# Attention forward and backward on one core: another hand-written order of units, other engines for some copies, 20 transposes ahead, last stores in halves

## The chip, the core and the metric

The kernel runs on one core of a Trainium2 chip. A core has a matrix engine (TensorE, "PE" in the profile; its weight loads are "PEld"), three engines for element-wise work (VectorE "DVE", ScalarE "ACT", GpSimd "POOL"), a queue engine that here does nothing but issue transfers (SyncE, "SP"), and sixteen DMA engines that carry out those transfers between the chip's HBM and the core's SBUF. Every transfer of this kernel is spread over all sixteen, eight partitions of a tile to each. TensorE writes to PSUM, 128 partitions by eight banks of 512 fp32 columns; VectorE and ScalarE read PSUM, GpSimd and the DMA engines don't.

The metric is the device time of one launch in microseconds. The kernel before takes 672.28 us, the median of eight runs.

## The reference, cut to what matters

Grouped-query attention for 32 batches, 32 query heads, 4 key/value heads, 4 queries per head, 2048 keys, head size 128, and its three gradients for a given output gradient:

```python
B, Hq, Hkv, Sq, Sk, D = 32, 32, 4, 4, 2048, 128

def _fwd_reference(q, k, v):
    k = jnp.repeat(k, rep, axis=1)          # rep = Hq // Hkv = 8
    v = jnp.repeat(v, rep, axis=1)
    scores = jnp.einsum("bhqd,bhkd->bhqk", q, k) * D ** -0.5
    p = jax.nn.softmax(scores, axis=-1)
    return jnp.einsum("bhqk,bhkd->bhqd", p, v)

def reference(q, k, v, grad_out):
    _out, _vjp = jax.vjp(_f, q, k, v)
    return (_out, *_vjp(grad_out))          # out, dq, dk, dv
```

The eight query heads of a key/value head, times four queries, are 32 rows; four key/value heads make 128 rows, one per partition. All arrays are bf16. Per batch K, V, dK and dV are 2 MiB each, the rest is small: 256 MiB of K, V, dK, dV plus 4 MiB of q, output gradient, output and dq cross the DMA engines, 260 MiB.

## The kernel before, in words

**Data.** On the host K and V are laid out as two arrays each, one for heads 0-1 and one for heads 2-3; a row of one partition holds 4096 bf16 values. K's rows carry 128 more, the q rows in the first array and the output gradient in the second (`LONG` = 4224 against `ROW` = 4096). So a batch loads four tiles, LK0, LK1 (1056 KB each), LV0, LV1 (1024 KB), and stores four, SV0, SV1 (dV) and SK0, SK1 (dK), of which SV1 and SK1 carry the output and dq in their last 128 columns. All tiles live in 20 SBUF buffers, `row0` to `row19` ("slots"), used for loads and stores alike. A load into a slot waits until the store from it has landed, or until TensorE has read the load that was there.

**Units.** The program is a list of units, each a short group of instructions of one engine. For a batch: transposes of q and the output gradient (QT, L230) and their copy out of PSUM (QTe); transposes of K and V, eight groups of four fp32 transposes each (KT, VT, L241: two neighbouring bf16 values travel as one fp32), and their copies to SBUF (KTe, VTe: ScalarE at L207, VectorE at L209); scores (S, L255, two halves into four banks); negative maximum (MX, VectorE, L260); exponential with row sums (EX, ScalarE, L264); reciprocal (RC, L268); three small GpSimd products (dop, qp, rs, L271 to L278); transposes of the exponentials (ET) and copies (ETe); output (O, L288) and its scaling (Oe, L294/L296); delta (DL, L299); DP (L255) and dS (DS, VectorE, L303); transposes of dS (DT, DTe); dq (DQ, L288, DQe L294/L296); dV and dK, eight units each, two matmuls into two banks (DV, DK, L310), and their casts into the store tiles (DVe, DKe, L316, ScalarE or VectorE).

**Order.** `PLAN` is one long string, four characters to a unit: the unit's kind (a letter, see `NAMES`), its part, its place (a PSUM bank, a slot, or "A"/"D" for ScalarE/VectorE) and a tile number. `plan()` reads it, counts the occurrences of a letter and part to get the batch, and `emit` writes the instructions in exactly that order under a manual schedule. Every engine works through its own units strictly in this order, and so does SyncE with the transfers: a transfer that must wait holds back all that follow it. The eight transfer semaphores are used in turn, so transfer n also waits until transfer n-8 has landed. The batches overlap: around the transposes of one batch stand dV and dK of the one before it, and loads run about three batches ahead.

In the middle of the run SyncE's order before is, for one batch, LK0.13, SK1.9, SV1.10, LV0.12, SV0.10, LK1.13, SK0.10, LV1.13 (kind, part, batch). Its end is LK0.31, SK1.27, SV1.28, LV0.30, SV0.28, LK1.31, SK0.28, LV1.31, SK1.28, SV1.29, LV0.31, and then eleven stores: SV0.29, SK0.29, SK1.29, SV1.30, SV0.30, SK0.30, SK1.30, SV1.31, SV0.31, SK0.31, SK1.31. The first batch's four loads are issued in halves (L225), heads first, in the order LK0, LK1, LV1, then LK0 of batch 1, LV0.

Of the kernel before, what the change touches and what calls it, by code (L numbers as in the profile page):

```python
# [14 lines left out]
P = 128  # L15
NH = 4
# [5 lines left out]

NAMES = dict(
# [5 lines left out]
    "a000a110b120a030b040a150e400f4A0e011f0A0e702f7A0e513f5A0b160a070e224f2A0e135f1D0c000d0D0e316f3A0g720h7A0e637f6A0"  # L29
    "b080a190g601h6D0g212h2A0i040i1-0j0D0g303h3A0e411f4A0e024f0A0g104h1D0k0A0g415h4D0g026h0D0l0D0e705f7A0e516p020q0A0"  # L30
    "f5D0b1a0p131q1D0m0-0A340B3A0A060B0D0A100B1A0a0d0r020r1-0s0D0t0D0o0-0A640B6A0A760B7D0u020v0D0g502h5A0A540B5A0E1c0"
    "b0e0A460B4A0e210f2D0e102f1D0c020d0D0e333f3A0A240B2A0E0b0u160v1D0g703h7A0e617f6A0n0-0C020D0D0C140D1A0C360D3D0a1h0"
    "g604h6A0g216h2A0i021i1-0j0D0C200D2A0g360h3A0e470f4A0w100x1A0k0A0g111h1D0g462h4D0g075h0D0C400D4D0w061x0A0l0D0e072"
    "f0A0C620D6A0F0f0C740D7D0e763f7A0e504p010q0A0f5D0b1i0p171q1D0m0-0A320B3A0A040B0D0A100B1A0a040r060r1-0s0D0t0D0A720"
    "B7D0o0-0A640B6A0u061v0D0g500h5A0y010C540D5A0y1-0z0D0F1g0A520B5A0E120b0c0A460e201f2A0B4D0e115f1D0c040d0D0e356f3A0"
    "A220B2A0E0j0u160v1D0g701h7A0e617f6A0n0-0C040D0D0C120D1A0C360D3D0a180g605h6A0g216h2A0i020i1-0j0D0C200D2A0g360h3A0"
    "e471f4A0w101x1A0g112h1D0k0A0g463h4D0g074h0D0C400D4D0w060x0A0l0D0e072f0A0C620D6A0F060C740D7D0e765f7A0e506p010q0A0"
    "f5D0b100p171q1D0m0-0A320B3A0A040B0D0A100B1A0a0g0r060r1-0s0D0t0D0o0-0A620B6A0A740B7D0y070C500D5A0y1-0z0D0F1b0u020"
    "v0D0g560h5A0A540B5A0E1f0b020A400B4D0e270f2A0e163f1A0c020d0D0e334f3D0A240B2A0E010u100v1D0g722h7A0e637f6A0n0-0C060"
    "D0D0C140D1A0C300D3D0a130g624h6A0g236h2A0i041i1-0j0D0C220D2A0g300h3A0C720e410f4A0w100x1A0g111h1D0k0A0g403h4D0g015"  # L40
    "h0D0C440D4A0w001x0D0l0D0D7A0e012f0D0C660D6A0F0a0e743f7D0e504p020q0A0f5D0b150p111q1D0m0-0A340B3A0A060B0D0A120B1A0"
    "a0b0r000r1-0s0D0t0D0o0-0A640B6A0A760B7D0y010C520D5A0y1-0z0D0F1j0u041v0D0g500h5A0A560B5A0E160b0f0A420B4D0e211f2A0"
    "e105f1A0c040d0D0e356f3D0A260B2A0E0e0u120v1D0g711h7A0e607f6A0n0-0C040D0D0C160D1A0C320D3D0a170g615h6A0g206h2A0i040"
    "i1-0j0D0C200D2A0g320h3A0e431f4A0w101x1A0g112h1D0k0A0g423h4D0g034h0D0C400D4D0w020x0A0l0D0e032f0A0C640D6A0F0i0C760"
    "D7D0e725f7A0e506p010q0A0f5D0b190p131q1D0m0-0A340B3A0A060B0D0A100B1A0a0j0r020r1-0s0D0t0D0o0-0A640B6A0A760B7D0y030"
    "C500D5A0y1-0z0D0F110u040v0D0g520h5A0A560B5A0E1a0b060A400B4D0e230f2A0e123f1A0c040d0D0e354f3D0A260B2A0E0c0u100v1D0"
    "g732h7A0e627f6A0n0-0C040D0D0C160D1A0C300D3D0a1h0g634h6A0g226h2A0i041i1-0j0D0C220D2A0g300h3A0e410f4A0w120x1A0g131"
    "h1D0k0A0g403h4D0g015h0D0C420D4D0w001x0A0l0D0e012f0A0C640D6A0F000C760D7D0e703f7A0e514p020q0A0f5D0b1e0p131q1D0m0-0"
    "A340B3A0A060B0D0A100B1A0a010r020r1-0s0D0t0D0o0-0A640B6A0A760B7D0y030C500D5A0y1-0z0D0F1d0u041v0D0g520h5A0A560B5A0"
    "E1i0b0a0A400B4D0e231f2A0e125f1A0c040d0D0e356f3D0A260B2A0E020u100v1D0g731h7A0e627f6A0n0-0C040D0D0C160D1A0C300D3D0"  # L50
    "a180g635h6A0g226h2A0i040i1-0j0D0C220D2A0g300h3A0e411f4A0w121x1A0g132h1D0k0A0g403h4D0g014h0D0C420D4D0w000x0A0l0D0"
    "e012f0A0C640D6A0F050C760D7D0e705f7A0e516p020q0A0f5D0b1f0p131q1D0m0-0A340B3A0A060B0D0A100B1A0a0d0r020r1-0s0D0t0D0"
    "o0-0A640B6A0A760B7D0y030C500D5A0y1-0z0D0F140u040v0D0g520h5A0A560B5A0E100b090A400B4D0e230f2A0e123f1A0c040d0D0e354"
    "f3D0A260B2A0E0c0u100v1D0g732h7A0e627f6A0n0-0C040D0D0C160D1A0C300D3D0a1g0g634h6A0g226h2A0i041i1-0j0D0C220D2A0g300"
    "h3A0e410f4A0w120x1A0g131h1D0k0A0g403h4D0g015h0D0C420D4D0w001x0A0l0D0e012f0A0C640D6A0F0i0C760D7D0e703f7A0e514p020"
    "q0A0f5D0b160p131q1D0m0-0A340B3A0A060B0D0A100B1A0a040r020r1-0s0D0t0D0o0-0A640B6A0A760B7D0y030C500D5A0y1-0z0D0F130"
    "u041v0D0g520h5A0A560B5A0E150b0e0A400B4D0e231f2A0e125f1A0c040d0D0e356f3D0A260B2A0E020u100v1D0g731h7A0e627f6A0n0-0"
    "C040D0D0C160D1A0C300D3D0a1b0g635h6A0g226h2A0i040i1-0j0D0C220D2A0g300h3A0e411f4A0w121x1A0g132h1D0k0A0g403h4D0g014"
    "h0D0C420D4D0w000x0A0l0D0e012f0A0C640D6A0F000C760D7D0e705f7A0e516p020q0A0f5D0b1a0p131q1D0m0-0A340B3A0A060B0D0A100"
    "B1A0a030r020r1-0s0D0t0D0o0-0A640B6A0A760B7D0y030C500D5A0y1-0z0D0F170u040v0D0g520h5A0A560B5A0E1i0b0f0A400B4D0e230"  # L60
    "f2A0e123f1A0c040d0D0e354f3D0A260B2A0E0c0u100v1D0g732h7A0e627f6A0n0-0C040D0D0C160D1A0C300D3D0a190g634h6A0g226h2A0"
    "i041i1-0j0D0C220D2A0g300h3A0e410f4A0w120x1A0g131h1D0k0A0g403h4D0g015h0D0C420D4D0w001x0A0l0D0e012f0A0C640D6A0F0h0"
    "C760D7D0e703f7A0e514p020q0A0f5D0b150p131q1D0m0-0A340B3A0A060B0D0A100B1A0a070r020r1-0s0D0t0D0o0-0A640B6A0A760B7D0"
    "y030C500D5A0y1-0z0D0F1j0u041v0D0g520h5A0A560B5A0E100b060A400B4D0e231f2A0e125f1A0c040d0D0e356f3D0A260B2A0E020u100"
    "v1D0g731h7A0e627f6A0n0-0C040D0D0C160D1A0C300D3D0a1e0g635h6A0g226h2A0i040i1-0j0D0C220D2A0g300h3A0e411f4A0w121x1A0"
    "g132h1D0k0A0g403h4D0g014h0D0C420D4D0w000x0A0l0D0e012f0A0C640D6A0F010C760D7D0e705f7A0e516p020q0A0f5D0b1i0p131q1D0"
    "m0-0A340B3A0A060B0D0A100B1A0a0j0r020r1-0s0D0t0D0o0-0A640B6A0A760B7D0y030C500D5A0y1-0z0D0F180u040v0D0g520h5A0A560"
    "B5A0E1h0b0a0A400B4D0e230f2A0e123f1A0c040d0D0e354f3D0A260B2A0E0c0u100v1D0g732h7A0e627f6A0n0-0C040D0D0C160D1A0C300"
    "D3D0a1f0g634h6A0g226h2A0i041i1-0j0D0C220D2A0g300h3A0e410f4A0w120x1A0g131h1D0k0A0g403h4D0g015h0D0C420D4D0w001x0A0"
    "l0D0e012f0A0C640D6A0F0d0C760D7D0e703f7A0e514p020q0A0f5D0b100p131q1D0m0-0A340B3A0A060B0D0A100B1A0a080r020r1-0s0D0"  # L70
    "t0D0o0-0A640B6A0A760B7D0y030C500D5A0y1-0z0D0F1g0u041v0D0g520h5A0A560B5A0E110b050A400B4D0e231f2A0e125f1A0c040d0D0"
    "e356f3D0A260B2A0E020u100v1D0g731h7A0e627f6A0n0-0C040D0D0C160D1A0C300D3D0a160g635h6A0g226h2A0i040i1-0j0D0C220D2A0"
    "g300h3A0e411f4A0w121x1A0g132h1D0k0A0g403h4D0g014h0D0C420D4D0w000x0A0l0D0e012f0A0C640D6A0F040C760D7D0e705f7A0e516"
# [87 lines left out]
def kernel(  # L161
# [36 lines left out]
    for u in units:  # L198
        if u.name in ("SV", "SK"):
            T[u.b]["D" + u.name[1], "out", u.part] = slots[int(u.where, 36)]  # L200
# [161 lines left out]
```

## Time and profile before, and how to read it

| | us |
|---|---|
| median of 8 runs (671.21 to 675.53) | 672.28 |
| the profiled execution, whole | 672.37 |
| its span (first to last instruction on the core) | 669.8 |
| TensorE busy / share | 610.2 / 91% |
| VectorE busy / share | 571.7 / 85% |
| ScalarE busy / share | 569.5 / 85% |
| GpSimd busy / share | 39.0 / 6% |
| HBM read / written | 136.31 MB / 136.31 MB |

Times in the profile count from the start of the span. Busy time is the union of an engine's instructions, so an engine can be busy nearly all the time and still not be what sets the end; a matmul's end is modelled. "PEclk" is the clock that TensorE was granted, in tenths of full speed. The costliest groups of the page, as line, engine, operation, out<-in, shapes, count | busy us, mean ns of one | idle before it, and what ended that:

```profile
L241 PE MATMUL psum<-ident,row 128*128 128x128 f32 x2048 | 292.0, 285 | 27.3 <-DMA row<-in_k_dram 19.5
L316 ACT CAST row<-psum 128x1024 bf16<-128x1024 f32 x292 | 289.5, 1024 | 31.2 <-PE psum L310 29.3
L316 DVE CAST row<-psum 128x1024 bf16<-128x1024 f32 x220 | 265.0, 1218 | 6.7 <-PE psum L310 3.8
L207 ACT COPY kt_sb<-psum 128x512 f32<-128x512 f32 x190 | 110.5, 599 | 21.4 <-PE psum L241 21.2
L303 DVE SCALAR_TENSOR_TENSOR ds_sb<-psum,delta,e_sb 128x1024 bf16<-128x1024 f32 x64 | 82.1, 1283 | 12.2 <-PE psum L255 7.5
```

The transfers, by what they write and read, with the size and the median time from issue to landing:

```profile
out_dram<-row SPq DMA_DIRECT2D x64, 1056.0 KB, 20.1
out_dram<-row SPq DMA_DIRECT2D x64, 1024.0 KB, 20.4
row<-in_k_dram SPq DMA_DIRECT2D x62, 1056.0 KB, 18.0
row<-in_v_dram SPq DMA_DIRECT2D x62, 1024.0 KB, 20.5
```

And what SyncE waited for, in total, times, longest:

```profile
SPq L320 <- DMA out_dram<-row: 124.1, 63, 2.2
SPq L226 <- DMA out_dram<-row: 106.1, 23, 5.6
SPq L320 <- DVE row L316: 87.2, 15, 9.7
SPq L226 <- DMA row<-in_v_dram: 83.6, 45, 2.1
```

### The profile page before, as it was taken

What the parts mean: (1) busy time and instruction counts of PE and PEld (TensorE: products, weight loads), DVE (VectorE), ACT (ScalarE), POOL (GpSimd) and SP (SyncE); (2) the same over time, 40 slices, a digit from 0 to 9 for tenths busy, and PEclk for the clock granted to TensorE, in tenths of its full rate; (3) what the DMA queues carried; (4) which work ended last, traced back from release to release, by engine and by line L of the source; (5) the groups of instructions that cost most, each with busy time, mean ns of one, the idle gap of its engine ahead of it and who ended that gap; (6) DMA issues with size and microseconds to landing.
All of it is one profiled execution on the core that took longest, in us unless ns stands there. A gap on an engine that the chain in (4) does not pass through costs nothing.

```text
span 669.8 us, 20678 instructions
## 1 busy us (share of the span) xinstructions
PE 610.2 (91%) x8768; PEld 403.8 (60%) x8768; DVE 571.7 (85%) x736; ACT 569.5 (85%) x802; POOL 39.0 (6%) x102
## 2 busy tenths in 40 slices
PE   6998999999998999989998989988999988898994
PEld 5665666666665666666655666655656665565652
DVE  1988899999997999979898889988789988887994
ACT  3987899999897899879888888987788988887894
POOL 0000000000000000000000000000000000000000
PEclk9999999999998999989999999999899999998997
DMA  9999999999999999999999999999999999999867
GB/s 352 420 423 422 427 400 421 423 424 423 424 425 424 423 425 424 423 425 419 408 420 424 413 413 409 408 420 421 417 420 412 416 419 422 399 421 424 353 251 322
DMA packets 37532, 273.96 MB, mean 409 GB/s; under 512 B 4160, under 2 KB 4160, under 8 KB 5184
## 3 DMA queue, kind: packets, MB, share of 16 engines
q1 hardware_dynamic: 37440, 272.65, 98.3%
q8 instruction: 68, 1.11, 0.6%
q14 instruction: 24, 0.20, 0.1%
HBM read 136.31 MB, written 136.31 MB: 407 GB/s over the span
## 4 chain that ended last, share of the span: by engine, by line
DMA 44%; PE 42%; ACT 5%; DVE 4%; issue 3%; SPq 0%; POOL 0%; DVEq 0%; ACTq 0%; POOLq 0%
DMA out_dram<-row 25%; PE psum L241 22%; DMA row<-in_k_dram 19%; PE psum L310 9%; PE psum L288 5%; PE psum L255 5%; ACT row L316 4%; DVE vt_sb L209 3%; DVE ds_sb L303 1%; DVE row L316 0%; PE psum L230 0%; ACT e_sb L264 0%; DVE e_sb L260 0%; ACT kt_sb L207 0%; ACT dt_sb L207 0%
## 5 line engine op out<-in xcount | busy, mean ns | idle before, releaser
L241 PE MATMUL psum<-ident,row 128*128 128x128 f32 x2048 | 292.0, 285 | 27.3 <-DMA row<-in_k_dram 19.5
L316 ACT CAST row<-psum 128x1024 bf16<-128x1024 f32 x292 | 289.5, 1024 | 31.2 <-PE psum L310 29.3
L241 PEld LDWEIGHTS psum<-ident,row 128*128 128x128 f32 x2048 | 226.5, 144 | 92.6 <-issue 32.6
L316 DVE CAST row<-psum 128x1024 bf16<-128x1024 f32 x220 | 265.0, 1218 | 6.7 <-PE psum L310 3.8
L207 ACT COPY kt_sb<-psum 128x512 f32<-128x512 f32 x190 | 110.5, 599 | 21.4 <-PE psum L241 21.2
L207 ACT COPY vt_sb<-psum 128x512 f32<-128x512 f32 x160 | 92.1, 603 | 33.8 <-PE psum L241 33.1
L303 DVE SCALAR_TENSOR_TENSOR ds_sb<-psum,delta,e_sb 128x1024 bf16<-128x1024 f32 x64 | 82.1, 1283 | 12.2 <-PE psum L255 7.5
L310 PE MATMUL psum<-ds_sb,qp_sb 32*128 32x512 bf16 x512 | 77.4, 386 | 3.4 <-ACT row L316 1.0
L260 DVE TENSOR_SCALAR_CACHE_REDUCE e_sb<-psum 128x2048 bf16<-128x2048 f32 x32 | 73.3, 2292 | 5.7 <-PE psum L255 5.7
L310 PE MATMUL psum<-e_sb,dop_sb 32*128 32x512 bf16 x512 | 69.0, 386 | 2.5 <-issue 1.1
L209 DVE COPY vt_sb<-psum 128x1024 bf16<-128x1024 bf16 x96 | 60.7, 684 | 10.3 <-PE psum L241 10.1
L209 DVE COPY kt_sb<-psum 128x1024 bf16<-128x1024 bf16 x66 | 45.0, 684 | 27.4 <-PE psum L241 27.1
L264 ACT ACTIVATE e_sb<-psum,m 128x2048 bf16<-128x2048 f32 x32 | 64.1, 2002 | 0.2 <-DVE e_sb L260 0.2
L271 POOL TENSOR_SCALAR dop_sb<-row,rinv 128x128 bf16<-128x128 bf16 x32 | 19.3, 602 | 603.9 <-DVE rinv L268 586.2
L241 PE MATMUL psum<-ident,ds_sb 128*128 128x128 f32 x256 | 42.2, 288 | 9.5 <-DVE vt_sb L209 7.0
L288 PE MATMUL psum<-row,dt_sb 128*32 128x128 bf16 x2048 | 44.0, 224 | 4.7 <-issue 4.6
L310 PEld LDWEIGHTS <-qp_sb 32*128 32x128 bf16 x512 | 19.4, 91 | 46.3 <-issue 42.9
L255 PE MATMUL psum<-vt_sb,qdt_sb 128*32 128x512 bf16 x512 | 40.1, 382 | 4.1 <-issue 4.1
L288 PEld LDWEIGHTS <-dt_sb 128*32 128x32 bf16 x2048 | 31.3, 96 | 20.8 <-issue 20.2
L241 PEld LDWEIGHTS psum<-ident,ds_sb 128*128 128x128 f32 x256 | 27.0, 141 | 27.2 <-DVE vt_sb L209 16.4
L207 ACT COPY dt_sb<-psum 128x512 f32<-128x512 f32 x63 | 38.3, 609 | 1.0 <-PE psum L241 0.9
L288 PEld LDWEIGHTS <-et_sb 128*32 128x32 bf16 x2048 | 30.4, 95 | 13.4 <-ACT et_sb L207 11.2
(29 smaller groups left out, 310.0 us busy)
## 6 DMA issues: line engine op xcount, KB each, us to landing
out_dram<-row SPq DMA_DIRECT2D x64, 1056.0 KB, 20.1
out_dram<-row SPq DMA_DIRECT2D x64, 1024.0 KB, 20.4
row<-in_k_dram SPq DMA_DIRECT2D x62, 1056.0 KB, 18.0
row<-in_v_dram SPq DMA_DIRECT2D x62, 1024.0 KB, 20.5
row<-in_v_dram SPq DMA_DIRECT2D x4, 512.0 KB, 9.6
row<-in_k_dram SPq DMA_DIRECT2D x2, 544.0 KB, 5.4
row<-in_k_dram SPq DMA_DIRECT2D x2, 512.0 KB, 4.5
```

Source lines behind the costliest of these rows:

```text
L207: nc.scalar.copy(out=out.bitcast(FP32), in_=in_)
L209: nc.vector.tensor_copy(out=out, in_=in_.bitcast(BF16))
L241: nc.tensor.transpose(out=ps[:, P * j:P * j + P], in_=src[:, 4 * half + j, :], identity=ident32[:])
L255: nc.tensor.matmul(out[r, QW * w:QW * w + QW], lhsT=t["qdt"][:, P * side + 32 * h:P * side + 32 * h + 32], rhs=t[x, NH * i + h][:, QW * w: ...
L260: nc.vector.tensor_scalar(out=t["e"][:], in0=t["S"], scalar1=-scale, scalar2=None, op0=ALU.mult, op1=ALU.min, accum_out=t["m"][:])
L264: nc.scalar.activation(out=t["e"][:], in_=t["S"], func=ACT.Exp, bias=t["m"][:], scale=scale, accum_out=t["l"][:])
L271: nc.gpsimd.tensor_scalar(out=t["dop"][:], in0=t["go"], scalar1=t["rinv"][:], scalar2=None, op0=ALU.mult)
L288: nc.tensor.matmul(t[name][r, :], lhsT=left[:, j, r, odd], rhs=right[:, 4 * i + j, :, odd], start=(i == 0 and c == 0), stop=(i == 1 and c ...
L303: nc.vector.scalar_tensor_tensor(out=t["ds"][:, w], in0=t["DP", i], scalar=t["dl"][:], in1=t["e"][:, w], op0=ALU.subtract, op1=ALU.mult)
L310: nc.tensor.matmul(acc[:, QW * (h % 2):QW * (h % 2) + QW], lhsT=t[still][rows[h], :], rhs=t[moving][rows[h], QW * i:QW * i + QW], start=Tr ...
L316: copy(out=heads_of(t[name[:2], "out", g])[:, :, QW * i:QW * i + QW], in_=t[name[:2], i, g].rearrange("p (h c) -> p h c", h=2))
```

## The change

The buffers, the tiles, the number and kind of units (but for the last stores) and the mathematics stay as they are. Five things change.

1. `PLAN` is another order. Units are moved one by one, on all engines. SyncE's order in the middle of the run becomes LK0.13, SK1.9, SV1.10, LK1.13, LV0.12, LV1.13, SV0.10, SK0.10. Its start is LK0.0, LV0.0, LK1.0, LV1.0, LK0.1, LK1.1, LK1.2, LK0.2, LV1.1, LK0.3, LV1.2, LV0.1, LV0.2, and only then the first store, SV0.0. Its end is LV0.30, SV0.28, LK1.31, SK1.27, SK1.28, LV1.31, LV0.31, SK0.28, SV1.28, SV1.29, SK0.29, SV0.29, SV0.30, SV1.30, SK0.30, SK1.29 and the last batch's stores with SK1.30 among them.
2. Copies out of PSUM change engines. For O and dq (Oe, DQe) 41 of 64 go from VectorE to ScalarE; V transposes' copies move by three to VectorE, K's by one to ScalarE, dK's casts by one to VectorE.
3. The store tiles have another layout, which the host undoes: a cast writes one run of 1024 columns where it wrote two runs of 512.
4. Twenty transposes of the identity come first on TensorE, into bank 7, which nothing reads.
5. The last batch's four stores are issued as two halves each (parts 2 to 5 of SV and SK); the first batch's loads are no longer split.

```diff
+LAST = 31
+WARM_UP = 20
...
 PLAN = (
-    "a000a110b120a030b040a150e400f4A0e011f0A0e702f7A0e513f5A0b160a070e224f2A0e135f1D0c000d0D0e316f3A0g720h7A0e637f6A0"
...
+    "F1c0u021v0D0g500h5A0A560B5A0E530A440B4D0A200B2D0E4a0E2a0u120v1D0C060D0D0C140D1A0C300D3A0C220D2A0w050x0A0w141x1A0"
+    "C400D4D0C660D6A0F290F3i0F490C720D7D0y040y1-0o0-0z0D0C500D5A0F5i0")
...
         u.name, u.part, u.b = NAMES[key[0]], int(key[1]), seen[key]
+        if u.name in ("SV", "SK") and u.part > 1:
+            u.b = LAST
...
         if u.name in ("SV", "SK"):
-            T[u.b]["D" + u.name[1], "out", u.part] = slots[int(u.where, 36)]
+            T[u.b]["D" + u.name[1], "out", u.part % 2] = slots[int(u.where, 36)]
...
-    heads_of = lambda row: row[:, 0:ROW].rearrange("p (h c) -> p h c", h=2)
...
-            for w in (slice(0, Sk), slice(Sk, n)) if b == 0 else (slice(0, n),):
-                nc.sync.dma_start(out=x[:, w], in_=src[:, w])
+            nc.sync.dma_start(out=x[:, 0:n], in_=src)
...
-            copy(out=heads_of(t[name[:2], "out", g])[:, :, QW * i:QW * i + QW],
-                 in_=t[name[:2], i, g].rearrange("p (h c) -> p h c", h=2))
+            copy(out=t[name[:2], "out", g][:, 2 * QW * i:2 * QW * i + 2 * QW], in_=t[name[:2], i, g])
         elif name in ("SV", "SK"):
-            n = LONG if i else ROW
-            nc.sync.dma_start(out=(dv_r if name == "SV" else dk_r)[i][b], in_=t["D" + name[1], "out", i][:, 0:n])
+            half, g = divmod(i, 2)
+            n = LONG if g else ROW
+            w = (slice(0, n), slice(0, ROW // 2), slice(ROW // 2, n))[half]
+            nc.sync.dma_start(out=(dv_r if name == "SV" else dk_r)[g][b][:, w], in_=t["D" + name[1], "out", g][:, w])
 
     with tc.manual_schedule():
+        for _ in range(WARM_UP):
+            nc.tensor.transpose(out=psum[:, QW * (BANKS - 1):QW * (BANKS - 1) + P], in_=ident32[:], identity=ident32[:])
         for u in units:
             emit(u)
...
-    return x.reshape(2, 32, P, 2, 8, P, 2).transpose(1, 0, 3, 5, 4, 6, 2).reshape(32, NH, 16 * P, P)
+    return x.reshape(2, 32, P, 4, 2, 2, P, 2).transpose(1, 0, 4, 6, 3, 5, 7, 2).reshape(32, NH, 16 * P, P)
```

## The prediction

> **What bounds the kernel now.** I read the page's slices first, then the chain of waits, the TensorE timeline, windows of the tail, and last the DMA view of ten microseconds near the end.
>
> ```profile
> DMA  9999999999999999999999999999999999999867
> GB/s 352 420 423 422 427 400 421 423 424 423 424 425 424 423 425 424 423 425 419 408 420 424 413 413 409 408 420 421 417 420 412 416 419 422 399 421 424 353 251 322
> ...
> q1 hardware_dynamic: 37440, 272.65, 98.3%
> ```
>
> The DMA engines have work in every slice but the last three. In the chain of waits, long stretches are nothing but transfers, end to end:
>
> ```profile
> 546.26 20.44 DMA out_dram<-row
> ...
> 566.78 20.51 DMA out_dram<-row
> ...
> 587.37 20.47 DMA out_dram<-row
> ```
>
> A link is 20.5 us because at most eight transfers are in flight: SyncE issues transfer n when n-8 has landed (a load landed at 584.70, the eighth after it was issued at 584.76). Eight transfers are one batch, so a batch takes 20.5 us. TensorE waits for that:
>
> ```profile
> 543.74 1.07 PE L241 MATMUL psum<-ident,row 128*128 128x128 f32 x8 [1.50 <-DMA row<-in_k_dram]
> 584.83 1.07 PE L241 MATMUL psum<-ident,row 128*128 128x128 f32 x8 [1.56 <-DMA row<-in_k_dram]
> ```
>
> Some 1.5 us per batch of compute slack. The end looks different:
>
> ```profile
> 620.00:630.00 10.00, 9.64 (x90) 6.75 (x87) 9.59 (x12) 9.45 (x16) 1.20 (x3) 1.00 0.93 392
> 630.00:640.00 10.00, 9.61 (x196) 5.65 (x196) 8.80 (x14) 8.71 (x13) 0.00 (x0) 1.00 0.82 335
> 640.00:650.00 10.00, 9.25 (x136) 6.11 (x137) 9.45 (x11) 9.44 (x14) 1.20 (x3) 1.00 0.48 197
> 650.00:660.00 10.00, 8.82 (x142) 4.19 (x142) 8.74 (x12) 9.31 (x12) 0.00 (x0) 0.91 0.84 344
> 660.00:670.00 10.00, 1.92 (x58) 1.10 (x46) 1.09 (x2) 1.44 (x2) 0.00 (x0) 0.67 0.64 265
> ```
>
> The DMA share (column before the last) leaves 0.7 + 1.8 + 5.2 + 1.6 + 3.6 = 12.9 us free, which reads as what earlier loads could win. The same 640 to 650 in quarter-microseconds says otherwise:
>
> ```profile
> DMA  9997999977999111000000000200000020009779
> GB/s 371 540 473 329 394 394 492 524 295 328 426 524 492 33 66 66 34 0 34 34 34 0 34 34 34 66 34 34 34 0 34 34 67 34 0 34 493 295 295 459
> ```
>
> From 643 to 649 one packet of 8 KB moves per 0.25 us: one engine of sixteen works off a backlog. The trace keeps an arrival event per engine and transfer, and they say the same: the store issued at 637.0 reached half its engines at 641.4 and the last at 650.3. This last engine falls behind all along: 1.9 us after the first at 50 us, 5.7 at 150, 13 from 320 on. Its arrivals from 150 to 625 us are apart, in the median, 2.45 us for a 1 MiB load, 2.59 for a 1 MiB store; the first engine's are 2.42 and 2.46. Its last arrivals are 628.21, 630.66, 633.77, 636.59, 638.99, 642.40, 644.73, 647.33, 650.25, 653.16, 655.72, 658.33, 661.10, 663.74, 666.18, 668.69: no hole in it. So the bound is this one late engine, from its first arrival (4.40) to its last (668.69): 664.3 us for 259.5 MiB, 2.56 us per MiB.
>
> The Trainium skill, "DMA: Bandwidth & Descriptors" (Latency and other measured facts), says engines 7 and 15 are usually slower, guesses at the descriptor rings of GpSimd's software path, and excludes the hardware path. The page's queue 1 is hardware and an engine is late, so the row decides; by the rule all engines would keep the first engine's pace, about 260 x 2.45 = 637 us, and the tail would count.
>
> **The change, part by part**, as microseconds on that engine. The run profiled took 672.37: span 669.8 (1.1 after the last arrival) and 2.6 around it; the median of eight is 672.28. I add to the median.
>
> *Bytes.* Same 260 MiB in 260 transfers (eight half loads fewer, four whole ones more; eight half stores for four whole). 0.
>
> *Order of the queue.* K heads 2-3 (LK1) move up by 1 to 3 MiB in most batches, V mostly by 1 to 4, dV/dK stores mostly back, by up to 4. Load after load goes from 39 pairs to 70, store after store from 39 to 74. On the late engine a 1056 KB load takes 2.551 after a load and 2.525 after a store; a 1056 KB store 2.679 after a store and 2.706 after a load. 31 x 0.026 - 31 x 0.027 = 0.
>
> *Loads close behind the store that frees their slot.* Before, never fewer than 7 places; after, 15 loads stand 2 to 6 places behind. SyncE stops at such a load, and all loads and stores behind it stop too, until the late engine has landed the store. At 2 places (once) one transfer of 2.5 us remains as cover. Issue to landing on an idle engine was at least 5.6 us (store at 652.72), against 5.0 of cover: 0.6 us; at 3 places the cover is 7.5: 0. Between 0 and 0.6; I take 0.3.
>
> *A dQ-carrying store ahead of the last loads.* dK heads 2-3 of batch 28 (SK1) goes from 245.8 to 242.8 MiB, in front of LV1 and LV0 of batch 31. It was issued at 612.85, as soon as its data were there; the late engine frees for that place at 623.1, and issue must lead by 2.4 us (first load: issued 0.72, landed 4.40, of which 1.28 transfer). 7.9 us of cover: 0. Without it, each microsecond of lateness is one.
>
> *First loads.* LK1 of batch 0 ends at 3.1 MiB instead of 2.1 (V comes between): it lands near 10.9 instead of 8.33, and batch 0's scores may slip by 2.5 us. Cover: 13.2 MiB of loads now stand ahead of the first store, which keeps the late engine busy to about 4.4 + 12.7 x 2.52 = 36.4; stores need issue by 34.0, and the first two were issued at 26.5 and 28.9. 0.
>
> *Warm-up.* Twenty transposes on TensorE before the first load, writing bank 7. Cold price of the first ones:
>
> ```profile
> 8.46 3.65 PE L241 MATMUL psum<-ident,row 128*128 128x128 f32 x16 [2.04 <-DMA row<-in_k_dram]
> 12.12 2.80 PE L241 MATMUL psum<-ident,row 128*128 128x128 f32 x20
> ```
>
> 228 ns each, then 140 (the windows' granted clock reads 1.00 in both, so only the durations show the step). 24 cold ones x 0.09 = 2.1 us saved, if they warm anything, under the loads: 0. The skill, "TensorE: Matmul & The Clock Gate" (Part 4), says transposes don't count as busy and won't raise the clock; the row, where nothing but transposes ran before the step, disagrees. By the rule nothing is saved; the sum is the same.
>
> *Single units on TensorE.* The clock falls to 0.83 in ten-microsecond windows such as 200-210, 470-480 and 610-620. Gone or not, TensorE's wait for loads covers it: 0.
>
> *Copies.* 41 evacuations of O and dQ (L296) go from VectorE to ScalarE; other moves come to -3 ScalarE copies net. ScalarE has no row for them: between VectorE's 0.35 us for the same tile and ScalarE's own 0.60 for 128x512; I take 0.35, since the tile is a quarter of that one. 41 x 0.35 less about 2.2 = +12 us over the run, at most +22, at 17.8 us busy per batch: 18.2 to 18.5, under 20.5. Output copies (L316) write one run of 1024 instead of two of 512; between 0.68 (VectorE's bf16 copy) and today's 1.22 on VectorE, 1.02 on ScalarE; I take today's. All beside the DMA: 0.
>
> *Last stores in halves, last loads earlier.* LV0 of batch 31 ends at 245.8 instead of 248.8 MiB, 7.6 us sooner; the last store is 0.53 MiB. Neither shortens the late engine's list. Its last fifteen arrivals took 40.5 us; at its own medians they are 2 x 2.45 + 6 x 2.59 + 7 x 2.69 (the 1056 KB stores) = 39.3. So 1.2 at most to win; eight halves cost 0.03 more each (2.55 against 2.49 per MiB at the start), +0.3. Bounds -1.2 and +0.3; I take -0.9, both together.
>
> *Scattered excess.* On the late engine some twenty transfers are 0.12 to 1.3 us late, 10.2 us in all. What strikes it may strike another engine in a changed order: half of it either way, -5 to +5. I take 0.
>
> Sum: 672.3 + 0.3 - 0.9 = 671.7. Range of this case: 667 to 676.5.
>
> **Rivals.** *The tail counts (faster).* If the late engine is no fixed property and the sixteen even out, compute sets the end. Both K loads of batch 30 stand at 233.6 MiB or less, where the late engine was at 600.1 instead of 605.2: 5.1 us sooner. The last issue moves from 662.5 to 657.4; half engines landed the last store 4.3 us after issue, less 1.25 for the half: 660.4, + 1.1 + 2.6 = 664.1. For it: the free share above. Against: 643 to 649. Chance 0.25.
>
> *ScalarE paces compute (slower).* Place: the evacuations from batch 1 on; price 0.38 us per batch. If ScalarE, not the loads, sets the rhythm, the end is 12 us late; the last half store needs issue by 665.0 (667.4 less 2.4) against 662.5, so it decides from 2.5 us on: 672.3 + 9.5 = 681.8. For it: 9.45 of 10 us busy in 620-630. Against: the 1.5 us waits for loads. Chance 0.10.
>
> *Excess falls on the late engine (slower by little)*: 672.3 + 2 to 4 = 675. Chance 0.12.
>
> **Numbers.** A measurement can tell 0.2%, 1.3 us. The forecast, that the late engine's list is as long as before, has 0.53; it splits into same 0.37, faster 0.15, slower 0.01; with the rivals: faster 0.40, same 0.37, slower 0.23. The range 664 to 676.5 reaches the first rival's time and leaves out the second; the likeliest case's own is 667 to 676.5.
>
> **What would show it.** Right: the late engine's arrivals without holes to the end at 2.45 and 2.59 per MiB, a last issue several microseconds before it must be, fewer single-engine slices or more without effect on the time. Wrong: arrivals of the last engine close to the others', its store price changed, a hole over 1 us in its list, or ScalarE busy without waits for loads.

## The result, and the profile after

The changed kernel is slower by half a per cent: 675.37 us in the median of 11 runs (673.43 to 679.63) against 672.3 (32 runs beside it), ratio 1.0052, 95% interval 1.0039 to 1.0066. The ratio counts a twelfth run of 676.93 us, with which the median is 675.82; so the change costs 3.1 us by the medians and 3.5 by the ratio. For the experiments below too, both measures are given where they differ. The execution profiled has a span of 674.9 us; before it was 669.8.

The page's slices of the kernel after, DMA share and rate, and the queue:

```profile
DMA  9999999999999999999999999889999979999978
GB/s 367 420 413 414 397 395 401 423 424 424 425 424 423 425 423 426 423 422 422 424 424 425 423 424 408 349 333 424 425 425 423 423 269 410 422 425 423 423 318 327
...
q1 hardware_dynamic: 37440, 272.65, 97.6%
```

Before, the rate fell below 360 GB/s in the first slice and at the very end only. Now there are two dips in the middle, in the 26th and 27th slice (422 to 456 us) and in the 33rd (540 to 557). What happened there is in SyncE's waits (in total, times, longest):

```profile
SPq L229 <- DMA out_dram<-row: 151.2, 26, 15.6
SPq L324 <- DVE row L319: 138.0, 29, 9.5
SPq L324 <- ACT row L297: 79.5, 19, 6.9
```

L229 is the load: 26 loads wait for a store to land, nearly all of them for the one that frees their slot, the longest for 15.6 us; before, it was 23 loads, and the longest such wait was 5.6. SyncE's timeline shows the longest one:

```profile
529.25 0.33 SPq L324 DMA_DIRECT2D out_dram<-row  x1
545.21 0.34 SPq L229 DMA_DIRECT2D row<-in_k_dram  x1
545.65 1.60 SPq L229 DMA_DIRECT2D row<-in_v_dram  x3
547.30 1.66 SPq L324 DMA_DIRECT2D out_dram<-row  x3
```

For 16 us nothing is issued. The load at 545.21 is LK0.28; it stands two places behind SK1.23, which frees its slot and landed at 545.2. Then eight transfers go out within 4 us. (The dip from 422 to 456 us has such a stop too: LK0.23, three places behind SK1.18, waits until 439.8, 15.5 us behind the issue before it.) The DMA view of 536 to 560 us, in slices of 0.6 us:

```profile
DMA  9999997652100000296999999999999999897899
GB/s 419 407 433 403 415 440 328 259 218 96 55 28 28 28 27 27 56 154 281 451 408 408 398 424 423 423 437 423 410 423 382 410 300 287 205 218 306 379 407 436
```

Three things are to be read here. From 540 on engine after engine runs dry, until from 543 to 546 one of sixteen is left (28 GB/s): the late engine, which still works off its backlog. Behind the restart all are busy again. And at 555 to 558 the share stays at 7 to 9 while the rate falls to 205: all sixteen engines are at work and move half as much. This third thing is nowhere in my prediction.

TensorE waits for what came late, in its timeline:

```profile
566.21 0.39 PE L313 MATMUL psum<-ds_sb,qp_sb 32*128 32x512 bf16 x4
570.05 1.09 PE L244 MATMUL psum<-ident,row 128*128 128x128 f32 x4 [3.45 <-DMA row<-in_k_dram]
```

That is its last wait for a load. From 572 us to the end the list of its waits has none (before, it had 2.2 us of them in that stretch):

```profile
PE psum L313 <- DVE row L319: 2.6, 5, 1.2
PE psum L313 <- issue: 1.3, 1, 1.3
PE psum L313 <- DVE ds_sb L306: 0.8, 1, 0.8
```

So the last hundred microseconds are paced by compute, and the chain of waits says so. Its last DMA link is the load that TensorE waited for (LK1.28, issued at 549.05); from its landing to the end there are compute links alone. (From 509 to 549 us too the chain runs through compute; the lines left out there are of TensorE and ScalarE.)

```profile
487.87 21.31 DMA out_dram<-row
...
549.05 20.87 DMA row<-in_k_dram
570.05 3.65 PE psum L244 x16
...
666.54 1.20 PE psum L291 x52
668.11 1.01 ACT row L319
```

The tail in windows (TensorE, its weight loads, VectorE, ScalarE, GpSimd busy; clock; DMA share; GB/s):

```profile
630.00:640.00 10.00, 8.93 (x186) 5.87 (x185) 6.52 (x11) 9.54 (x16) 1.42 (x4) 1.00 1.01 423
640.00:650.00 10.00, 9.79 (x88) 6.21 (x87) 9.31 (x12) 9.10 (x14) 0.00 (x0) 1.00 0.91 378
650.00:660.00 10.00, 7.77 (x182) 4.53 (x180) 8.23 (x11) 7.66 (x12) 1.21 (x3) 1.00 0.71 289
660.00:670.00 10.00, 6.33 (x96) 3.26 (x88) 6.91 (x7) 6.24 (x8) 0.00 (x0) 0.83 1.01 403
670.00:675.00 5.00, 0.00 (x0) 0.00 (x0) 0.00 (x0) 0.00 (x0) 0.00 (x0) 0.52 0.34 132
```

The DMA share no longer falls to 0.48 at 640 to 650, since the late engine's lag was lost in the stop (it landed SK1.23 7.6 us behind the first engine, and LK0.28, the next but one, 0.9 us behind); it falls to 0.71 at 650 to 660, where now even the last engine waits: the store issued at 652.4 finds all engines idle, and the late engine's arrivals have a hole of 2.3 us there and one of 1.2 us at the store issued at 658.6. The last store is issued at 669.1 (before 662.5) and has landed at 673.8 (before 668.7).

Two measures go through all experiments below. The first is the start of the exponential of a batch (EX31: of batch 31), one per batch. The second is the late engine's list: when the last of the sixteen engines has landed the first so many MiB of the list, against the kernel before. Both are read from the trace's records, one execution each. The records don't name the engines: that the last arrival is always the same engine's is inferred from the stretches in which one engine alone is at work. ("Late loads back", "last compute", "both" and "queue of before" are experiments that follow.)

```
MiB landed             30     110     170     180     205     220     250    259.5    EX28   EX31  last issue
before, us           79.1   286.9   438.6   464.5   527.7   565.7   642.8   667.5   580.3  644.7   662.5
changed kernel       +2.1    -3.3    -0.5    +0.6    +1.5    +3.3    +2.1    +4.6   588.2  648.7   669.1
late loads back      +2.3    -2.7    -2.7    -3.0    -1.9    -1.9    -2.7    -0.9   582.3  642.9   664.1
last compute         +2.5    -4.0    -2.7    -1.8    -0.5    +1.9    +0.3    +1.9   586.7  645.8   664.6
both                 +1.9    -3.2    -1.7    -2.2    -1.2    -1.2    -1.9    -1.6   583.0  642.0   659.1
queue of before      +2.2    +3.2    +4.5    +3.8    +4.4    +4.4    +3.2    +5.7   585.0  647.7   669.1
```

How far single executions scatter can be seen at 160 MiB: up to there the changed kernel and five of the experiments below have the same units and the same list, and they lie 0.5 to 2.8 us ahead of the kernel before. So what a row gains or loses over a stop says more than the difference of two rows.

The changed kernel is ahead of the kernel before by 3 us at 110 MiB. It loses 1.1 us at the first stop (170 to 180 MiB, 424 to 440 us), 1.8 at the second (205 to 220), and 2.5 in the tail.

### The profile page after: what moved, and what is told of

Same layout as the page of the kernel before. It is cut to its first block, busy times and chain, and to the rows that moved or that the text cites. A ratio compares the mean times of both kernels' runs of the same rounds, so it can differ in the third digit from the quotient of the medians.

```text
span 674.9 us, 20652 instructions
## 1 busy us (share of the span) xinstructions
PE 614.1 (91%) x8788; PEld 404.3 (60%) x8788; DVE 560.3 (83%) x698; ACT 576.8 (85%) x840; POOL 39.0 (6%) x102
## 4 chain that ended last, share of the span: by engine, by line
PE 28%; DMA 19%; ACT 4%; DVE 4%; issue 2%; DVEq 0%; SPq 0%; ACTq 0%
DMA out_dram<-row 16%; PE psum L244 14%; PE psum L313 6%; PE psum L291 4%; PE psum L258 3%; ACT row L319 3%; DMA row<-in_k_dram 3%; DVE vt_sb L214 2%; DVE row L319 1%; DVE ds_sb L306 0%; DVE e_sb L263 0%; ACT vt_sb L212 0%; ACT e_sb L267 0%; PE psum L233 0%; ACT row L297 0%
## 5 line engine op out<-in xcount | busy, mean ns | idle before, releaser
L319 ACT CAST row<-psum 128x1024 bf16<-128x1024 f32 x291 | 290.4, 1024 | 52.4 <-PE psum L313 40.1
L244 PEld LDWEIGHTS psum<-ident,row 128*128 128x128 f32 x2048 | 222.7, 142 | 82.3 <-issue 31.3
L306 DVE SCALAR_TENSOR_TENSOR ds_sb<-psum,delta,e_sb 128x1024 bf16<-128x1024 f32 x64 | 82.1, 1283 | 30.0 <-PE psum L258 16.9
L313 PE MATMUL psum<-ds_sb,qp_sb 32*128 32x512 bf16 x512 | 79.6, 388 | 7.1 <-ACT row L319 2.7
L214 DVE COPY vt_sb<-psum 128x1024 bf16<-128x1024 bf16 x99 | 62.7, 684 | 9.7 <-PE psum L244 9.6
L313 PEld LDWEIGHTS <-dop_sb 32*128 32x128 bf16 x512 | 16.7, 92 | 44.0 <-issue 29.4
## 6 DMA issues: line engine op xcount, KB each, us to landing
row<-in_v_dram SPq DMA_DIRECT2D x64, 1024.0 KB, 17.8
```

Of the source, the lines that this page charges most:

```text
L214: nc.vector.tensor_copy(out=out, in_=in_.bitcast(BF16))
L244: nc.tensor.transpose(out=ps[:, P * j:P * j + P], in_=src[:, 4 * half + j, :], identity=ident32[:])
L306: nc.vector.scalar_tensor_tensor(out=t["ds"][:, w], in0=t["DP", i], scalar=t["dl"][:], in1=t["e"][:, w], op0=ALU.subtract, op1=ALU.mult)
L313: nc.tensor.matmul(acc[:, QW * (h % 2):QW * (h % 2) + QW], lhsT=t[still][rows[h], :], rhs=t[moving][rows[h], QW * i:QW * i + QW], start=Tr ...
L319: copy(out=t[name[:2], "out", g][:, 2 * QW * i:2 * QW * i + 2 * QW], in_=t[name[:2], i, g])
```

## The experiments

Each ran beside the kernel before, on the same chip; the four rounds ran on three chips, and the kernel before took 671.8 to 672.4 us in them. LK0.28 is the load of K's heads 0-1 of batch 28, SK1.23 the store of dK's heads 2-3 of batch 23; the diffs show SyncE's list in this notation where only the list is changed. Theory Q puts the loss into the order of SyncE's list, theory C into the order and the engines of the compute units.

**The cross: compute units and list exchanged.** First the changed kernel's compute with the list of before, then the reverse.

```diff
-LK0.13 SK1.9 SV1.10 LK1.13 LV0.12 LV1.13 SV0.10 SK0.10
+LK0.13 SK1.9 SV1.10 LV0.12 SV0.10 LK1.13 SK0.10 LV1.13
...
```

> The changed kernel's compute units, in their order and on their engines, with the list of transfers of the kernel before (its order, its slots, its split first loads, its whole last stores); the warm-up stays. Theory Q (the order of SyncE's list costs the 3.1 us: loads 2 to 3 places behind the store that frees their slot, SK1.28 ahead of the last V loads, the order of the last stores): the time falls back to that of the kernel before, 672.3 us, within 1. Theory C (the order and the engines of the compute units cost it, in the last batch above all, where EX31 to the last store's issue took 20.4 us instead of 17.8): the time stays at 674.5 to 675.5. Half and half would be 673.8.

Measured: 677.1 us, ratio 1.0067 (1.0041 to 1.0093).

> The other half of the same cross: the compute units of the kernel before, in their order and on their engines, without warm-up, with the changed kernel's list of transfers, half stores and single first loads among it. Theory Q: 675 us, as the changed kernel. Theory C: 672.3 us or, with the halves at the end, up to 1.2 below it (671.1).

Measured: 679.56 us, ratio 1.0110 (1.0089 to 1.0132).

Both theories missed both. The first mixture is slower than the kernel before and no faster than the changed one (their intervals overlap); the second is slower than both. So neither the new list nor the new compute order is made good by its old counterpart. In the first one the loss lies at the start: batch 1's and batch 2's stores come ready later in the new compute order, and the old list makes SyncE wait for them in front of loads (stores that the kernel before issues at 58.9, 64.0 and 82.1 us go out at 61.6, 69.6 and 86.1). The DMA view of 50 to 100 us, in slices of 1.25 us, of that kernel:

```profile
DMA  9999999999999999999999989999569999999999
GB/s 432 399 433 426 403 416 308 367 427 421 424 425 408 419 427 447 418 412 426 433 358 356 355 223 380 433 426 403 222 264 420 229 380 426 364 216 250 399 433 419
```

The late engine is 4.3 us behind the kernel before at 35 MiB, and 4.4 at 220: without slack in its list, a loss at 80 us is still there at 570. Another 2.5 us come between 250 MiB and the end, as in the changed kernel. In the second mixture both stops stand as in the changed kernel (EX28 at 588.9), and the store SK0.30 leaves a hole of 4.2 us in the late engine's list.

**The late loads moved back.** From batch 21 on, each load that stands less than seven places behind the store that frees its slot goes to the seventh place. The two that matter:

```diff
-SK1.18 SV0.19 SK0.19 LK0.23 LV0.22 LK1.23 SK1.19 SV1.20
+SK1.18 SV0.19 SK0.19 LV0.22 LK1.23 SK1.19 SV1.20 LK0.23
...
-SK1.23 SK0.24 LK0.28 LV0.27 LV1.27 LV1.28 SK1.24 SV1.25
+SK1.23 SK0.24 LV0.27 LV1.27 SK1.24 LV1.28 SV1.25 LK0.28
```

> The changed kernel; from batch 21 on each load that stood less than 7 places behind the store that frees its slot is moved back to the seventh place (LK0.23 by four places, LK0.28 by five, six others by one). SyncE should not stand still from 424 to 440 and from 529 to 545 us any more. Theory Q: EX28 comes 3 to 5 us earlier than the changed kernel's 588.2, and the time falls by 2 to 3 us, to 672.5 to 673.4. Theory C, and the view that the late DMA engine had its lag to give away in the stops: 674.9 to 675.4, no change.

Measured: 671.62 us, ratio 0.9990 (0.9974 to 1.0007). The intervals of this and of the changed kernel are apart: the stops cost 675.37 - 671.62 = 3.7 us (4.2 by the ratios), more than the whole loss. The DMA view of the same 24 us as above, 536 to 560:

```profile
DMA  9999999899999999999999999899999999999999
GB/s 427 441 442 414 371 384 343 329 438 398 373 405 433 379 435 432 389 401 414 429 429 431 404 432 436 379 448 431 426 412 427 442 419 434 392 419 414 427 440 414
```

No engine runs dry, and no stretch of half rate follows. EX28 comes 5.9 us earlier, and the late engine loses 0.8 us from 170 to 220 MiB, where the changed kernel loses 3.8. The clock granted to TensorE does not explain the loss: its mean over the runs is 0.977 in the changed kernel and 0.980 here, against 0.984 in the kernel before beside this run, which is no faster than this one.

**One load alone.** Only LK0.28 goes back, to the seventh place.

```diff
-SK0.24 LK0.28 LV0.27 LV1.27 LV1.28 SK1.24 SV1.25 SV0.25
+SK0.24 LV0.27 LV1.27 LV1.28 SK1.24 SV1.25 LK0.28 SV0.25
```

> The changed kernel, one transfer moved: LK0.28 five places back, behind SV1.25 (two places behind the store of its slot before, seven after). Theory Q with the stop at 529 to 545 us as the larger one (the late engine's lead over the kernel before went from -0.6 to +1.9 us there in the run with the last batch's order, 2.5 us, and from -2.7 to -1.1 at the stop of 424 to 440): 672.9 us. If both stops are needed, since the second makes up for what the first leaves: 674.5 or more.

Measured: 672.40 us, ratio 1.0017 (1.0001 to 1.0032). One transfer five places back is worth 3.0 us by the medians and 2.4 by the ratios; the intervals of the two kernels are apart. The stop at LK0.23 is still in: the late engine goes from -1.7 at 170 MiB to -0.5 at 180.

**The reverse, in the kernel before.** The same load five places forward, so that it stands two places behind its store.

```diff
-SK1.23 SV1.24 LV0.26 SV0.24 LK1.27 SK0.24 LV1.27 LK0.28
+SK1.23 SV1.24 LK0.28 LV0.26 SV0.24 LK1.27 SK0.24 LV1.27
```

> The reverse in the kernel before: LK0.28 five places forward, so that it stands two places behind SK1.23, which frees its slot; nothing else. Theory Q: SyncE stands still until SK1.23 has landed (some 13 us), the late engine gets its next transfers late, and the time rises by 2 to 2.5 us, to 674.3 to 674.8. The prediction's term (at most 0.6 for all such loads together): 672.3 to 672.9.

Measured: 673.97 us, ratio 1.0034 (1.0022 to 1.0046), 2.2 us above the kernel before. SyncE's timeline and the DMA view of 524 to 548 us (0.6 us to a slice):

```profile
513.04 2.59 SPq L320 DMA_DIRECT2D out_dram<-row  x2
533.09 0.34 SPq L226 DMA_DIRECT2D row<-in_k_dram  x1
533.52 0.38 SPq L226 DMA_DIRECT2D row<-in_v_dram  x1
```

```profile
DMA  5654411000010000648999999997799999999999
GB/s 253 253 253 210 183 70 55 28 28 28 28 42 14 28 28 28 99 127 352 408 408 380 412 355 273 259 205 191 328 437 423 437 443 421 422 422 406 439 423 410
```

The same picture: dry to one engine, a restart, and 5 us later a stretch with all engines busy at 191 to 273 GB/s. On the late engine LK0.28 itself arrives on time (2.51 us per MiB behind the transfer before it); the next load, LV0.26, is 1.7 us late, in that stretch.

**How close is too close.** The same load four, then five places behind its store; and two places behind, with a store as the next transfer.

```diff
-SK1.23 SV1.24 LV0.26 SV0.24 LK1.27 SK0.24 LV1.27 LK0.28
+SK1.23 SV1.24 LV0.26 SV0.24 LK0.28 LK1.27 SK0.24 LV1.27
...
+SK1.23 SV1.24 LV0.26 SV0.24 LK1.27 LK0.28 SK0.24 LV1.27
...
+SK1.23 SV1.24 LK0.28 SV0.24 LV0.26 LK1.27 SK0.24 LV1.27
```

> The kernel before, LK0.28 three places forward, four places behind SK1.23. Two places behind it cost 2.2 us, although the late engine's list had no hole of note there (2.51 us per MiB for LK0.28); the 1.7 us came in the next load, in a stretch of 3 us in which all sixteen engines moved half as much. Theory R (what costs is the restart: the fifteen other engines run dry whenever SyncE stops, and behind the restart loads run at half rate for a while): they run dry here too, +1.5 to +2.2, 673.5 to 674.3. Theory H (what costs is the late engine's own wait, which three more transfers ahead of LK0.28 cover): 672.0 to 672.5.

Measured: 674.06 us, ratio 1.0028 (1.0018 to 1.0039).

> The same with LK0.28 five places behind SK1.23. Theory R: the other engines run dry for some 3 us only, +0 to +1.5. Theory H: 0, 672.0 to 672.5. If the cost falls place by place from 2.2 us at two: 0.9 us, 673.1.

Measured: 673.25 us, ratio 1.0018 (1.0006 to 1.0031).

> The kernel before with LK0.28 two places behind SK1.23, and LV0.26 behind SV0.24, so that the transfer behind the restart is a store. If only loads suffer behind a restart and the stretch is bound to its time: the late engine's 1.7 us go, and what is left is LV0.26's own lateness, 672.5 to 673.3. If a restart costs the same whatever follows: +2.2 or more, 674 to 675.

Measured: 675.21 us, ratio 1.0041 (1.0027 to 1.0056).

Four places behind, the late engine still has three transfers to do when SyncE starts again, and the cost is still 1.8 us; five places behind it is 1.0. Each is clear of zero; that the cost falls with the distance is likely and not shown, since the intervals overlap. Theory H, the late engine's own wait, which is how my prediction had priced it, is refuted: a store that is waited for costs time although the late engine has work. Theory R came true in its times. Of its two parts, the half rate behind the restart is in all four traces; that the engines must have run dry is not shown, since at five places they still moved 238 GB/s or more while SyncE waited. The DMA view of 524 to 548 us with four places:

```profile
DMA  9999988555544210937999999988999999999999
GB/s 402 444 443 400 414 372 343 233 247 247 233 178 178 110 55 28 197 70 323 379 436 436 436 436 322 224 197 280 370 396 424 438 438 438 438 398 434 393 436 436
```

Again half rate behind the restart, at 538.4 to 541. With a store next the cost does not go (2.9 us against 2.2, in intervals that overlap): the late engine is 1.3 us late at LK0.28 and 1.3 at SV0.24, and LV0.26, one place later, holds compute up (EX27 at 567.9 instead of 559.8). Whether loads alone suffer is not settled by it.

**The last batch's compute units as before.** Everything behind EX30 stands in the order and on the engines of the kernel before; the list stays. An excerpt, with the engine behind the colon:

```diff
-DT0.31 DTe0.31:A DT1.31 DTe1.31:A DK4.31 DKe4.31:D DK6.31 DKe6.31:A DK7.31 DKe7.31:D DQ0.31 DQ1.31 rs0.31 DQe0.31:D DK5.31 DKe5.31:A
+DT1.31 DTe1.31:A DK4.31 DKe4.31:D DT0.31 DTe0.31:A DK6.31 DKe6.31:A DK7.31 DKe7.31:D DQ0.31 DK5.31 DKe5.31:A DQ1.31 DQe0.31:D
...
```

> The changed kernel; the compute units behind EX30 stand in the order and on the engines of the kernel before (batch 30's second half and batch 31), the list of transfers is the changed kernel's. Theory C in its narrow form (the last batch's units cost 2.6 us): EX31 to the last store's issue falls from 20.4 to about 17.8 us, the time to 672.8. Theory Q: the holes at 652 and 658 us stay, 674.5 to 675.4.

Measured: 674.25 us, ratio 1.0029 (1.0014 to 1.0044). EX31 to the last issue takes 18.8 us instead of 20.4, not 17.8; 1.1 us less in the median, with an interval that touches the changed kernel's.

**Both undone.** The diffs of the late loads and of the last batch together.

> The changed kernel with both edits of the runs before: the loads from batch 21 on at the seventh place behind their stores, and the compute units behind EX30 in the order and on the engines of the kernel before. If the stops and the last batch are two causes that add (3.7 us and 1.1 us measured alone), the time is 670.5 us, below the kernel before. If the list of the late DMA engine is the only bound once the stops are gone, the last batch's order adds nothing: 671.6.

Measured: 670.00 us, ratio 0.9982 (0.9967 to 0.9997): a version that beats both kernels, the old one by 0.2%. Against the late loads alone the last issue is 5.0 us earlier (659.1 against 664.1) and the last landing only 0.6 us (667.1 against 667.7): in these two executions the late engine's list is the bound again once the stops are gone, and compute that ends sooner finds it busy. The times don't settle it. By the medians the last batch's order adds 1.6 us, as if the two causes summed up (670.5 was expected of that), by the ratios 0.5 us, and the intervals overlap. Windows of the tail:

```profile
640.00:650.00 10.00, 9.30 (x186) 5.98 (x185) 9.26 (x14) 9.87 (x13) 1.21 (x3) 1.00 0.61 247
650.00:660.00 10.00, 6.77 (x106) 3.22 (x106) 7.45 (x8) 8.08 (x10) 0.00 (x0) 1.00 1.01 406
660.00:670.00 10.00, 0.00 (x0) 0.00 (x0) 0.00 (x0) 0.00 (x0) 0.00 (x0) 0.50 0.51 202
```

Compute is done at 660 and the DMA engines work for another 7 us; at 640 to 650 the share of 0.61 is the late engine's backlog, as in the kernel before.

**The compute of before with the mended list.** The fourth corner of the cross: the changed kernel's list with the diff of the late loads, all compute units in the old order and on the old engines, no warm-up.

> The compute units of the kernel before (order and engines, no warm-up) with the changed kernel's list of transfers in which the loads from batch 21 on are moved back to the seventh place behind their stores: the fourth corner, against 679.6 us with the list as changed. Theory Q: the stops were what this compute order suffered from too, and the time falls by 4 or more, to 675 or less; if the late engine's list is then the only bound, to 670 to 672. If the compute order of before simply doesn't fit this list (its stores come ready in another order, as the hole of 4.2 us ahead of SK0.30 in that run): 677 to 679.

Measured: 674.00 us, ratio 1.0031 (1.0011 to 1.0051), against 679.56 with the list as changed. The stops cost this compute order 5.6 us. What keeps it 2.4 us above the changed kernel's compute with the same list is not settled; its late engine is 3.5 us ahead of the kernel before at 110 MiB and even at 170.

**The moved copies, back on their engines.** 58 copies, 41 of them O's and dQ's; once with the stops in, once with the late loads back.

```diff
-s0A0
+s0D0
...
-z0A0
+z0D0
...
```

> The changed kernel with each of its 58 moved copies back on the engine that it had (29 DQe and 12 Oe from ScalarE back to VectorE among them); order, list and all else as changed. The prediction's term for the copies was 0: 675.4 us, within 0.7. If ScalarE's 16 us more of work held compute up from batch 28 to the end, where no load is waited for any more: 673 to 674.

Measured: 676.49 us, ratio 1.0079 (1.0054 to 1.0104), against 1.0052 with the copies moved.

> The changed kernel with the late loads at the seventh place (671.6 us with nothing else undone) and each moved copy back on the engine that it had (1.1 us slower than the changed kernel where the stops were in, with intervals that touch). If the copies on ScalarE are a gain of their own: 672.3 to 673. If they are covered, as the prediction had them: 671.3 to 672.

Measured: 672.74 us, ratio 1.0012 (0.9995 to 1.0028), against 0.9990. Both times 1.1 us slower with the copies back by the medians (1.8 and 1.5 by the ratios); the intervals overlap in both, so a gain of one to two microseconds by ScalarE is likely and not shown. Both speak against ScalarE as a new bound.

**SK1.28 behind the last V loads.**

```diff
-SK1.27 SK1.28 LV1.31 LV0.31 SK0.28
+SK1.27 LV1.31 LV0.31 SK1.28 SK0.28
```

> The changed kernel with SK1.28 two places back, behind LV1.31 and LV0.31, which SyncE then issues without waiting for batch 28's last copies. The prediction's term: 0, 675.0 to 675.7. If the standstill of 605 to 618 us is a stop like the others: 672.9 to 673.5.

Measured: 675.02 us, ratio 1.0048 (1.0027 to 1.0068): nothing, although SyncE stands still for 13 us there in the changed kernel.

**Halves in the kernel before.**

```diff
-SV1.31 SV0.31 SK0.31 SK1.31
+SV3.31 SV5.31 SV4.31 SV2.31 SK2.31 SK3.31 SK4.31 SK5.31
```

> The compute units and the list of transfers of the kernel before, split first loads included; only the four stores of the last batch go in halves, in the changed kernel's order (the store tiles are laid out as in the changed kernel; its evacuations take 1024 ns on ScalarE and 1219 on VectorE, as before). The prediction's term: 0.9 us less, 671.1 to 671.4 (its bounds: 670.9 to 672.6). If the end is the late engine's list, whatever the size of the pieces: 672.

Measured: 672.11 us, ratio 0.9990 (0.9979 to 1.0000), 0.3 us below the kernel before by the medians and 0.7 by the ratio. The interval, from -1.4 to 0 us, holds both expectations.

**Without the warm-up.**

```diff
-WARM_UP = 20
+WARM_UP = 0
```

> The changed kernel without its 20 transposes ahead of the first load's arrival. The prediction's term: 0, 675.0 to 675.7. If the TensorE clock matters at the start: 1 us later, 676.4.

Measured: 675.38 us, ratio 1.0037 (1.0025 to 1.0048): no effect that can be told. TensorE's first work on a load, with the twenty transposes and without them:

```profile
1.60 3.86 PE L328 MATMUL psum<-ident 128*128 128x128 f32 x20 [1.60 <-DVE ident L192]
5.64 0.66 PE L244 MATMUL psum<-ident,row 128*128 128x128 f32 x4 [0.18 <-DMA row<-in_k_dram]
```

```profile
5.67 1.09 PE L244 MATMUL psum<-ident,row 128*128 128x128 f32 x4 [5.67 <-DMA row<-in_k_dram]
```

The transposes do warm: four take 0.66 instead of 1.09 us, and the eight behind them 1.09 instead of 1.97. EX0 starts at 20.2 instead of 21.1, and the loads cover it.

## Why the prediction missed

The forecast was no change, 671.7; the time lies 3.7 us above it. What failed is one step, *Loads close behind the store that frees their slot*: "0 and 0.6; I take 0.3". It measured 3.7 us. The place, the distances of two and three and SyncE's standstill were named rightly; the price was taken from the wrong thing. I asked only whether the late engine finds its next transfer in time, and it does: LK0.28 reaches it 0.35 us late two places behind the store, LK0.23 with no delay three behind. (The 5.6 us of issue to landing "on an idle engine" were misread as well: at 652.72 the late engine was still busy with the store before, and the others landed this one 3.8 to 4.0 us behind its issue. With that the term would have been 0.) Three things were left out.

- *The other fifteen engines.* They run ahead of the late one, so they have nothing left long before the store lands on it: at SK1.23 by 7 to 13 us in the kernel before and by 4.5 to 7.6 in the changed one. My sum has no term for their idling.
- *The restart.* Behind it comes a stretch of 1.5 to 3 us at half rate, in which the late engine loses 1 to 2 us where the load stood two to four places behind. At LK0.23 that is all that it loses. Five places behind the store still cost 1.0 us, in a list without slack. The stretch is in the traces; what makes it is open.
- *What stands behind the stopped load.* LV0.27, LV1.27, LV1.28 and LK1.28 were held back with LK0.28. Batch 28 starts 4 to 6 us late (EX28 at 588.2 against 582.3 with the loads back), and the 1.5 us per batch of slack, which I had read from waits up to 584.83, are used up. From there compute sets the end, and two of the prediction's own signs of being wrong are in the trace: holes of over 1 us in the late engine's list, at 652 and 658 us, and a last engine close to the others, 2 us behind the first at 600 us instead of 13.

The other steps:

- *Last stores in halves, last loads earlier*, -0.9: not settled. The halves alone gave 0.3 us by the medians, in an interval that holds 0 and -0.9; the earlier loads were not tried alone. But in the changed kernel the last batch's units came in an order that issues the last store 5 us later than the old order does (664.1 against 659.1 with the loads back). I costed the last batch's stores and not the units that produce them; in time that is 0.5 to 1.6 us, in intervals that overlap.
- *A dQ-carrying store ahead of the last loads* (SK1.28), 0, and *Warm-up*, 0: right, by a run each. For the warm-up I had set the row (228 ns falling to 140) against the Trainium skill, "TensorE: Matmul & The Clock Gate" (Part 4), which says that the clock gate does not count transposes as busy in the same way. The two timelines above side with the row, 0.66 against 1.09 us.
- *Copies*, 0: right in that ScalarE paces nothing; they may even be worth 1.1 to 1.8 us. O's and dQ's scaling takes 0.38 us on ScalarE, where I took 0.35.
- *Order of the queue* and *Scattered excess*, 0: over the first 170 MiB the list ends up 0.5 us ahead, after 3.3 us at 110; the scatter of single executions is as large.
- *First loads*, 0: not tried alone; at 20 us EX0 is 1.9 us late, and at 110 MiB the list is ahead. The stop at LK0.5 (52 to 64 us, three places behind its store) was not taken out either; it leaves the late engine 2.1 us behind at 30 MiB, which it has made up by 60.

The rivals: of "the tail counts" the time did not come, 664.1, and its condition came by another way. The late engine is no accident (at 400 us the last engine lands a transfer 7 to 13 us behind the first in every run); but the stop at 529 us let it catch up, the sixteen stayed close, and compute did set the end, only later and not sooner. "Excess falls on the late engine", +2 to 4 with 0.12, is nearest to what came, but its cause was not chance.

The terms as measured, by the medians: stops +3.7 (shown), last batch's order +1.1 to 1.6, moved copies about -1.1, halves -0.3 (none of these three clear of noise); 3.1 is the measured whole, so some -0.5 is left for all the rest. The sum is rough, since terms that share one bound need not add.

## What to carry to other kernels

When a hand-written transfer order is changed, look at each load's distance from the store that frees its buffer before anything else: here, with eight transfers in flight, the kernel before keeps seven places throughout and the mended list from batch 21 on; one load at five places cost 1.0 us, and at two places 2 to 3 us of 675. (Six was not tried alone, and that the number of transfers in flight sets the distance is an inference from this one case.) Price a stop of the queue by everything behind it, not by the bottleneck's own next transfer: which engines run dry, what the restart costs, and which later loads arrive late together. And test a new compute order and a new transfer order together: neither half with the other's old counterpart was faster here than either original.

## What the runs showed of the hardware

When SyncE had stood still for a store and then issued five to eight transfers within 4 us, there was a stretch of 1.5 to 3 us, starting 3 to 10 us after the first new issue, in which at least 13 of the sixteen engines were busy and they moved some 200 instead of 420 GB/s. Counted as microseconds with at least 13 engines busy and under 300 KB moved, by the packet records: past the first 10 us the kernel before has such a stretch at 90 us, the changed one at 67, 100, 110, 447 and 555 among others. All four runs with LK0.28 put forward in the kernel before have one between 536.5 and 541 us, and the kernel before has none there. All six kernels with the changed kernel's stop at LK0.28 (the changed one and five of the experiments) have one at 552 to 559 us, and none of the eight in which that load stands seven places behind has one from 540 to 600.

That the engines have run dry is not what it takes: at 67 us in the changed kernel and at 90 in the kernel before, SyncE had stood still for 11 us or more, but the DMA engines were busy throughout. Those at 100 and 110 us come with no standstill of over 8 us in the 30 us before them. What makes the stretch I don't know. That the engines start in step, or that many transfers are issued at once, are guesses that no run tells apart; ahead of the one at 67 us only three had been issued within 4 us.

The instruction queue moves data as well: 69 packets of 16 KB, each some 0.95 us long, about one every 10 us. The records do not tell on which engine, so whether they have a share in the scattered lateness of single engines stays open.
